# V's heads loaded alternately through SyncE's and ScalarE's queues

## Chip, cores, metric

One core of a Trainium2 chip. The metric is the device time of one execution in microseconds (us). Times inside a trace are us from the start of the span, which is what the profile covers of the execution; the span of the kernel before is 84.0 in an execution of 85.8. "Clock" is the clock that TensorE (PE in the views) was granted, as a share of its full speed.

## The reference

One decode step of a transformer block for 4 sequences: a layer norm whose scale and shift come from a condition, attention of 32 query heads over the last 1024 positions of a K and a V cache with 8 heads, and a feed-forward part, each with a residual.

```python
# B=4, D=512, Hq=32, Hkv=8, Dh=128, Dff=1792; W = 1024 positions of the cache are used
mod = (silu(c) @ w_mod).reshape(4, 6, 1, -1)           # sa, ca, ga, sb, cb, gb
h = layernorm(x) * (1 + ca) + sa
q = (h @ wq) as (B, Hq, 1, Dh)
p = softmax(q @ k[:, :, -W:].T * Dh ** -0.5)           # each K and V head serves 4 query heads
x = x + ga * ((p @ v[:, :, -W:]) as (B, 1, Hq*Dh)) @ wo
h = layernorm(x) * (1 + cb) + sb
x = x + gb * (relu(h @ w1) @ w2)
```

All inputs are bf16. K and V are 8 MB each, wq and wo 4 MB each, w_mod 3 MB, w1 and w2 1.75 MB each (MB of 2^20 bytes): 30.5 MB in all are read once for very little arithmetic.

## The kernel before

All large loads are written down first, all through SyncE's queue. K comes in eight tiles of 1 MB (k0 to k7), V in eight heads of 1 MB (v0 to v7). K and V share a pool of 11 buffers, so v3 and later need a buffer that a K tile has left. SyncE is not in the set of engines whose order is fixed by hand.

```python
ctx.enter_context(tc.manual_schedule(engines={PE, Activation, DVE, Pool}))        # names shortened
kvpool = ctx.enter_context(tc.tile_pool(name="kvpool", bufs=11))
...
nc.scalar.dma_start(out=cx_sb[0:B, :], in_=c)
nc.scalar.dma_start(out=cx_sb[B:2 * B, :], in_=A_x.rearrange("b o d -> (b o) d"))
... # through nc.sync: k0, k1, w_mod, wq (2 loads), k2 .. k7
for h in range(Hkv):
    vt_ = kvpool.tile([P, NI, Dh], bf16, tag="kv", name=f"v{h}")
    nc.sync.dma_start(
        out=vt_[:].rearrange("p j d -> p (j d)"),
        in_=A_v_cache[:, h, S - W:, :].rearrange("b (p j) d -> p b (j d)", j=NI),
    )
    v_tiles.append(vt_)
... # through nc.sync: wo (4 loads), w1, w2 (5 loads)
```

The compute stages that matter here, in the order of the text. `k_transposes` turns one K tile on TensorE and copies it out of PSUM (where this kernel has TensorE's results), two of four pieces on ScalarE and two on VectorE. The V products (`pv`) take the heads in the order 0 to 7 (the first three interleaved).

```python
for gi in range(KAHEAD, NG):                      # KAHEAD = 2, NG = 8
    if gi + 1 < NG:
        kts_pending.append(k_transposes(gi + 1))
    k_scores(gi, kts_pending.pop(0))
...
for iq in range(NQ):                              # four exponentials on ScalarE
    nc.scalar.activation(out=e_sb[:, ws]..., in_=sc_ps[:, ws]..., func=ACT.Exp, bias=nb[:], scale=scale, ...)
... # p_rep on VectorE; pT by TensorE, copied out half by ScalarE and half by VectorE
for iq in range(NQ):
    for h in range(VEARLY):                       # VEARLY = 3
        pv(h, iq * IQ, (iq + 1) * IQ, first=(iq == 0 and h == 0))
for h in range(VEARLY, Hkv):
    pv(h, 0, NI, last=(h == Hkv - 1))
... # o, products with wo, layer norm, products with w1 and w2, out
```

## Time and profile before

| | before |
|---|---|
| time, median of 4 runs | 85.91 us (85.75 to 86.06) |
| span of the profiled run | 84.0 us |
| mean rate over the span | 381 GB/s read from HBM |
| queue of SyncE / of ScalarE | 31.99 MB (of 10^6 bytes: the same 30.5) in 4196 packets / 0.01 MB in 16 packets |
| last large transfer done | near 80.1 us |
| last V product done | 62.73 us |

The table is read in one way: the transfers run without a gap from 2 us to 80 us (on the page the DMA share is 0.8 or more in every slice from 2.1 to 77.7, and the last chain is transfers for 92%), and the arithmetic follows them closely. The lines behind it are in the prediction.

### The profile page before, as it was taken

To read this page: it belongs to the slowest core of one execution; us is meant where nothing else is said; L and a number is where in the kernel's file an instruction comes from. 1 tells how busy PE (TensorE), PEld (TensorE's weight loads), DVE (VectorE), ACT (ScalarE), POOL (GpSimd) and SP (SyncE) were. 2 spreads that over 40 slices of the span, in tenths; PEclk is the share of its full clock that TensorE was granted. 3 is DMA by queue.
4 is the path that set the end of the run, shared out by engine and by line. 5 is a ranking of instruction groups with operands and counts; after the bars stand their busy time and mean duration, and the time that the engine had idled before them with its cause. 6 is when DMAs were issued, how large, how long until landed. Compare 5 with 4: busy or idle time off the path is not lost.

```text
span 84.0 us, 2368 instructions
## 1 busy us (share of the span) xinstructions
PE 57.2 (68%) x1064; PEld 46.8 (56%) x1064; DVE 26.3 (31%) x73; ACT 23.5 (28%) x37; POOL 5.2 (6%) x20
## 2 busy tenths in 40 slices
PE   0039930599629899999999239996455478598730
PEld 0039920238529749977777039996452058588510
DVE  0145470030430103654666677500003020241320
ACT  2314760003020004977789096300000010011000
POOL 6980000000000000000000000000000000000000
PEclk9999999858955555999999995795555555555555
DMA  0999998999989999999999999999999999999600
GB/s 2 329 406 452 456 480 374 429 444 429 437 374 417 417 441 409 409 413 433 425 406 413 425 429 417 409 425 429 413 409 413 429 419 443 417 376 401 236 4 2
DMA packets 4221, 32.14 MB, mean 382 GB/s; under 512 B 492, under 2 KB 628, under 8 KB 1140
## 3 DMA queue, kind: packets, MB, share of 16 engines
q1 hardware_dynamic: 4196, 31.99, 91.9%
q8 instruction: 8, 0.13, 0.6%
q10 hardware_dynamic: 16, 0.01, 0.0%
q14 instruction: 1, 0.01, 0.0%
HBM read 31.99 MB, written 0.00 MB: 381 GB/s over the span
## 4 chain that ended last, share of the span: by engine, by line
DMA 92%; SPq 2%; PE 1%; DVE 1%; issue 0%
DMA v<-in_A_v_cache_dram 28%; DMA wo_sb<-in_A_wo_dram 24%; DMA wq_sb<-in_A_wq_dram 21%; DMA w<-in_B_w_dram 19%; SPq L81 1%; PE z_ps L470 1%; SPq L90 1%; DVE zg L480 0%; DVE res L482 0%
## 5 line engine op out<-in xcount | busy, mean ns | idle before, releaser
L207 ACT COPY kT<-ktp 128x1024 bf16<-128x1024 bf16 x16 | 15.5, 1016 | 12.7 <-PE ktp L202 11.7
L202 PEld LDWEIGHTS <-k 128*128 128x128 bf16 x256 | 17.0, 108 | 3.7 <-issue 2.5
L202 PE MATMUL ktp<-ident_k,k 128*128 128x128 bf16 x256 | 18.0, 238 | 1.1 <-DMA k<-in_A_k_cache_dram 1.1
L205 DVE COPY kT<-ktp 128x1024 bf16<-128x1024 bf16 x16 | 11.1, 691 | 11.1 <-PE ktp L202 10.8
L340 PE MATMUL oT_ps<-pT,v 128*128 128x16 bf16 x256 | 7.3, 172 | 2.5 <-issue 1.9
L340 PEld LDWEIGHTS <-v 128*128 128x128 bf16 x256 | 7.1, 100 | 2.7 <-issue 2.0
L214 PE MATMUL sc_ps<-kT,qpad 128*32 128x512 bf16 x64 | 5.6, 445 | 0.4 <-DVE qpad L306 0.4
L357 PE MATMUL pT_ps<-ident_bf,p_rep 128*128 128x128 bf16 x32 | 3.3, 289 | 2.9 <-DVE p_rep L351 2.9
L357 PEld LDWEIGHTS <-p_rep 128*128 128x128 bf16 x32 | 2.9, 135 | 3.4 <-DVE p_rep L351 3.2
L236 PE MATMUL m_ps<-wmod_sb,siluT 128*32 128x512 bf16 x16 | 1.5, 516 | 4.5 <-DMA wmod_sb<-in_w_mod_dram 4.5
L302 PE MATMUL qT_ps<-hT,wq_sb 128*128 128x4 bf16 x128 | 3.6, 166 | 1.4 <-DVE ab L295 1.4
L302 PEld LDWEIGHTS <-wq_sb 128*128 128x128 bf16 x128 | 3.5, 104 | 1.5 <-issue 1.5
L409 ACT COPY y<-y_ps 128x256 f32<-128x256 f32 x1 | 0.4, 372 | 11.4 <-DVE y L408 11.4
L404 PE MATMUL y_ps<-wo_sb,o 128*32 128x512 bf16 x16 | 2.1, 620 | 2.0 <-DMA wo_sb<-in_A_wo_dram 1.1
L177 PE MATMUL tp<-ident_bf,cx_sb 8*128 8x8 bf16 x4 | 0.3, 167 | 4.5 <-DMA cx_sb<-in_A_x_dram 4.5
L236 PEld LDWEIGHTS <-siluT 128*32 128x32 bf16 x16 | 0.4, 107 | 4.8 <-issue 4.6
L382 DVE TENSOR_TENSOR oT_sb<-oT_ps,rb 128x128 bf16<-128x128 f32 x1 | 0.3, 292 | 8.6 <-PE oT_ps L340 8.6
L416 PEld LDWEIGHTS <-wo_sb 128*128 128x128 bf16 x64 | 2.5, 120 | 0.6 <-DMA wo_sb<-in_A_wo_dram 0.6
L416 PE MATMUL y_ps<-o,wo_sb 128*128 128x4 bf16 x64 | 2.4, 173 | 0.5 <-DMA wo_sb<-in_A_wo_dram 0.5
L351 DVE TENSOR_TENSOR p_rep<-e_sb,mi 128x512 int32<-128x512 int32 x4 | 2.5, 686 | 0.7 <-ACT e_sb L346 0.7
L470 PE MATMUL z_ps<-w,uT 128*32 128x128 bf16 x56 | 2.2, 302 | 0.7 <-DMA w<-in_B_w_dram 0.5
L177 PEld LDWEIGHTS <-cx_sb 8*128 8x128 bf16 x4 | 0.2, 108 | 4.5 <-issue 4.5
(107 smaller groups left out, 56.1 us busy)
## 6 DMA issues: line engine op xcount, KB each, us to landing
k<-in_A_k_cache_dram SPq DMA_DIRECT2D x8, 1024.0 KB, 26.2
v<-in_A_v_cache_dram SPq DMA_DIRECT2D x8, 1024.0 KB, 19.9
wq_sb<-in_A_wq_dram SPq DMA_DIRECT2D x2, 2048.0 KB, 20.7
wo_sb<-in_A_wo_dram SPq DMA_DIRECT2D x4, 1024.0 KB, 19.9
wmod_sb<-in_w_mod_dram SPq DMA_DIRECT2D x1, 3072.0 KB, 13.5
w<-in_B_w_dram SPq DMA_DIRECT2D x1, 1792.0 KB, 21.7
w<-in_B_w_dram SPq DMA_DIRECT2D x2, 512.0 KB, 19.2
w<-in_B_w_dram SPq DMA_DIRECT2D x1, 384.0 KB, 17.8
```

The lines of the kernel that those rows point to most:

```text
L202: nc.tensor.transpose(out=tp[:, ii, :], in_=k_tiles[gi][:, iq * IQ + ii, :], identity=ident_k)
L205: nc.vector.tensor_copy(out=dst, in_=tp[:])
L207: nc.scalar.copy(out=dst, in_=tp[:])
L214: nc.tensor.matmul(out=sc_ps[hw * CG:(hw + 1) * CG, half * HALF:(half + 1) * HALF], lhsT=qpad[:, b, par, hw, :], rhs=kT[:, half * (NI // 2 ...
L236: nc.tensor.matmul(out=m4_ps[k * CG:(k + 1) * CG, :], lhsT=siluT32[:, t, :], rhs=wmod_sb[:, t, k * D:(k + 1) * D], start=(t == 0), stop=(t ...
L302: nc.tensor.matmul(out=qT_v[:, hq, :], lhsT=wq_sb[:, t, hq * Dh:(hq + 1) * Dh], rhs=hT[:, t, :], start=(t == 0 and hq == 0), stop=(t == DT ...
L340: nc.tensor.matmul(out=oT_ps[:, hw, par].rearrange("p b r -> p (b r)"), lhsT=v_tiles[h][:, i, :], rhs=pT[:, i, c0:c0 + B * rep], start=(fi ...
L351: nc.vector.tensor_tensor(out=p_w[:, ws, :], in0=e_w[:, ws].unsqueeze(2).to_broadcast([P, WQ // 2, B]), in1=mi4[:].unsqueeze(1).to_broadca ...
L357: nc.tensor.transpose(out=tp[:, ii, :], in_=p_rep[:, i // 2, :, i % 2], identity=ident_bf[:])
L404: nc.tensor.matmul(out=y4_ps[q0:q0 + CG, :], lhsT=o4[:, l, g % 2, g // 2, :], rhs=wo_sb[:, g, l, :], start=(g == 0 and l < 4), stop=(g == ...
L416: nc.tensor.matmul(out=y_ps[:, m, :], lhsT=wo_sb[:, g, l, m::DT], rhs=o4[:, l, g % 2, g // 2, 0:B], start=False, stop=(g == NP - 1 and l = ...
L470: nc.tensor.matmul(out=z_ps[nh * CG:(nh + 1) * CG, :], lhsT=uT32[:, m, :], rhs=w2_sb[:, m, nh * DH2:(nh + 1) * DH2], start=(m == 0), stop= ...
```

## The change

The intent is to spread V's loads over two issuing engines. Even heads stay with SyncE, odd heads go to ScalarE. ScalarE's instructions are fixed in the order of the text, so its issues need places there: after the copies of k5, k6 and k7, and after the exponentials. SyncE joins the engines of fixed order, and the loads of wo, w1 and w2 move behind V in the text.

```diff
-        ... PE, Activation, DVE, Pool}))
+        ... PE, Activation, DVE, Pool, SP}))
     v_tiles = []
-    for h in range(Hkv):
+
+    def load_v(h, eng):
         vt_ = kvpool.tile([P, NI, Dh], bf16, tag="kv", name=f"v{h}")
-        nc.sync.dma_start(
+        eng.dma_start(
     ... (the loads of wo, w1, w2 leave this place)
     for gi in range(KAHEAD, NG):
         if gi + 1 < NG:
             kts_pending.append(k_transposes(gi + 1))
+
+        if gi >= NG - 4 and gi + 1 < NG:
+            h = 2 * (gi - NG + 4)
+            load_v(h, nc.sync)
+            load_v(h + 1, nc.scalar)
         k_scores(gi, kts_pending.pop(0))
     ... (after the four exponentials)
+    load_v(Hkv - 2, nc.sync)
+    load_v(Hkv - 1, nc.scalar)
+    ... (the loads of wo, w1, w2 unchanged, through nc.sync)
```

More of the change, by code (lines that the diff above doesn't have):

```diff
@@ L59 @@
     ctx.enter_context(tc.manual_schedule(engines={
-        mybir.EngineType.PE, mybir.EngineType.Activation, mybir.EngineType.DVE, mybir.EngineType.Pool}))
+        mybir.EngineType.PE, mybir.EngineType.Activation, mybir.EngineType.DVE, mybir.EngineType.Pool, mybir.EngineType.SP}))
     const = ctx.enter_context(tc.tile_pool(name="const", bufs=1))
@@ L109 @@
     NP = Hkv // 2
-    wo_sb = wts.tile([P, NP, NL, D], bf16, tag="big", name="wo_sb")
-    wo_src = A_wo.rearrange("(g p l) n -> p g (l n)", g=NP, l=NL)
-    wo_dst = wo_sb[:].rearrange("p g l n -> p g (l n)")
-    for g in range(NP):
-        nc.sync.dma_start(out=wo_dst[:, g, :], in_=wo_src[:, g, :])
-    w12 = wts.tile([P, DT * Dff + FT * D], bf16, tag="med", name="w12")
-    w1_sb = w12[:, 0:DT * Dff].rearrange("p (t n) -> p t n", t=DT)
-    w2_sb = w12[:, DT * Dff:DT * Dff + FT * D].rearrange("p (m n) -> p m n", m=FT)
-    nc.sync.dma_start(out=w1_sb, in_=B_w1.rearrange("(p t) n -> p t n", t=DT))
-    W2_CHUNKS = [(0, 4), (4, 4), (8, 3), (11, 2), (13, 1)]
-    assert sum(e for _, e in W2_CHUNKS) == FT
-    w2_dst = w12[:, DT * Dff:DT * Dff + FT * D]
-    for (m0, e) in W2_CHUNKS:
-        nc.sync.dma_start(out=w2_dst[:, m0 * D:(m0 + e) * D],
-                          in_=B_w2[m0 * P:(m0 + e) * P, :].rearrange("(q e) n -> q (e n)", e=e))
     nc.scalar.preload_act_table_set("natural_log_exp_and_others")
@@ L348 @@
                              bias=nb[:], scale=scale, accum_out=den4[:, iq:iq + 1])
+    load_v(Hkv - 2, nc.sync)
+    load_v(Hkv - 1, nc.scalar)
+    wo_sb = wts.tile([P, NP, NL, D], bf16, tag="big", name="wo_sb")
+    wo_src = A_wo.rearrange("(g p l) n -> p g (l n)", g=NP, l=NL)
+    wo_dst = wo_sb[:].rearrange("p g l n -> p g (l n)")
+    for g in range(NP):
+        nc.sync.dma_start(out=wo_dst[:, g, :], in_=wo_src[:, g, :])
+    w12 = wts.tile([P, DT * Dff + FT * D], bf16, tag="med", name="w12")
+    w1_sb = w12[:, 0:DT * Dff].rearrange("p (t n) -> p t n", t=DT)
+    w2_sb = w12[:, DT * Dff:DT * Dff + FT * D].rearrange("p (m n) -> p m n", m=FT)
+    nc.sync.dma_start(out=w1_sb, in_=B_w1.rearrange("(p t) n -> p t n", t=DT))
+    W2_CHUNKS = [(0, 4), (4, 4), (8, 3), (11, 2), (13, 1)]
+    assert sum(e for _, e in W2_CHUNKS) == FT
+    w2_dst = w12[:, DT * Dff:DT * Dff + FT * D]
+    for (m0, e) in W2_CHUNKS:
+        nc.sync.dma_start(out=w2_dst[:, m0 * D:(m0 + e) * D],
+                          in_=B_w2[m0 * P:(m0 + e) * P, :].rearrange("(q e) n -> q (e n)", e=e))
     for iq in range(NQ):
```

## The prediction

> **What bounds the kernel now.** I read the chain that ended last first, as the page sums it up and then in order of time (start, duration, what; all times in us from the span's start unless ns is said).
>
> ```profile
> DMA 92%; SPq 2%; PE 1%; DVE 1%; issue 0%
> ...
> 20.50 23.76 DMA v<-in_A_v_cache_dram
> ...
> 44.28 19.86 DMA wo_sb<-in_A_wo_dram
> ...
> 64.16 15.96 DMA w<-in_B_w_dram
> ```
>
> The end is set by transfers: 92% of the span is one chain of them. No engine is in it for over 2%. Next I read the span in four stretches (start:end, length, busy of PE, PEld, DVE, ACT, POOL with counts, PE clock, DMA share, GB/s).
>
> ```profile
> 20.50:44.30 23.80, 21.12 (x363) 17.31 (x364) 8.88 (x23) 10.15 (x13) 0.00 (x0) 0.78 1.01 419
> 44.30:64.20 19.90, 13.40 (x361) 11.95 (x358) 7.84 (x16) 6.13 (x13) 0.00 (x0) 0.74 1.01 419
> ```
>
> The transfer engines are full (share 1.0) at 419 GB/s while K's second part and V arrive. The bytes are the same after the change, so it can gain only if the rate rises. Then I read the issues in SyncE's queue, one window at a time (start, issue time).
>
> ```profile
> 4.41 0.60 SPq L81 DMA_DIRECT2D k<-in_A_k_cache_dram  x1
> 5.83 1.18 SPq L81 DMA_DIRECT2D k<-in_A_k_cache_dram  x2
> ...
> 20.50 0.54 SPq L101 DMA_DIRECT2D v<-in_A_v_cache_dram  x1
> 26.89 0.54 SPq L101 DMA_DIRECT2D v<-in_A_v_cache_dram  x1
> 29.37 0.54 SPq L101 DMA_DIRECT2D v<-in_A_v_cache_dram  x1
> 41.83 0.54 SPq L101 DMA_DIRECT2D v<-in_A_v_cache_dram  x1
> 44.28 0.33 SPq L114 DMA_DIRECT2D wo_sb<-in_A_wo_dram  x1
> ```
>
> An issue takes 0.54, but the next waits. v0 is issued at 20.50 and lands 23.76 later, at 44.26; wo's first part, the eighth load after v0, is issued at 44.28. So **a load is issued when the load eight places before it has landed**: there are eight in flight. In steady state one lands every 2.48 (26.89 to 29.37), which is 1.05 MB at 423 GB/s. By this rule k2 to k7 land at 29.37, 31.91, 34.38, 36.87, 39.36, 41.83, and v7 at 61.7. The count runs over both queues: k4 goes out at 5.83, when k0 lands, which is eight places back only if ScalarE's two small loads (c, x) are counted alternately with SyncE's, in the order c, k0, x, k1. That is an order planned by time, not the order of the text.
>
> Last, what TensorE does with the V heads and after (start, duration, in brackets the idle time before it and its releaser).
>
> ```profile
> 43.59 1.96 PE L202 MATMUL ktp<-ident_k,k 128*128 128x128 bf16 x32
> 45.48 1.25 PE L214 MATMUL sc_ps<-kT,qpad 128*32 128x512 bf16 x16
> 52.76 3.45 PE L340 MATMUL oT_ps<-pT,v 128*128 128x16 bf16 x128
> 61.71 1.02 PE L340 MATMUL oT_ps<-pT,v 128*128 128x16 bf16 x32 [0.59 <-DMA v<-in_A_v_cache_dram]
> 64.48 1.05 PE L404 MATMUL y_ps<-wo_sb,o 128*32 128x512 bf16 x8 [0.89 <-DVE o L395]
> 66.66 1.05 PE L404 MATMUL y_ps<-wo_sb,o 128*32 128x512 bf16 x8 [1.14 <-DMA wo_sb<-in_A_wo_dram]
> 71.64 1.23 PE L416 MATMUL y_ps<-o,wo_sb 128*128 128x4 bf16 x32 [0.48 <-DMA wo_sb<-in_A_wo_dram]
> 75.96 1.89 PE L459 MATMUL u_ps<-ab,w 128*128 128x8 bf16 x56 [0.43 <-DMA w<-in_B_w_dram]
> ```
>
> At every stage TensorE waits a little for data. Those waits are the slack in which a delay can be lost.
>
> [...] 0.54 of issue lies beside 2.48 of transfer, so there is no issue time to save. [...]
>
> **The change part by part.** *SyncE* loses four V loads and its order becomes that of the text: k0 to k7, v0, v2, v4, v6, wo, w1, w2. That costs nothing. *ScalarE* gains four issues. Its own two in the trace took 0.55 and 0.26; with 0.54 each that is 2.2, of which 1.6 lies in the K stage. There ScalarE copies 1.93 in every 2.48, which leaves 0.55, about one issue: hidden. *Bytes and rate* are unchanged: the last transfer still lands near 80.1, if the queues never run dry.
>
> *Order of arrival* is what moves. [...] v1 is reached soon after the two small activations at 24.4. Suppose first that the count follows the pairs (v0, v1, v2 ...). v1 then waits for wq's second half (26.89), v3 for k3, v5 for k5, v7 for k7. [...] the pair takes 2 x 2.48 = 4.96. Then: k2 and v1 at 31.85, k3 at 34.33, k4 and v3 at 39.29, k5 at 41.77, k6 and v5 at 46.73, k7 at 49.21. So **k7 lands 7.4 later**, behind three odd heads. From there:
> - k7's transposes to the last score took 3.14 (43.59 to 46.73): scores done at 52.4 (before 46.73, so +5.7; the 1.7 by which TensorE lagged behind k7 is taken up).
> - Scores to the first V product is 6.03 (46.73 to 52.76): 58.4. The V products without their waits are 5.35 + 1.08 + 1.02 = 7.45: done at 65.9, before 62.73. All V has landed by 61.7 as now, so these wait for nothing: **+3.2**.
> - The first wo product starts 1.75 later (67.65), and its two blocks take 2.1: 69.75 (before 67.71, +2.05, since wo's second part was waited for and now is not). To the second wo group 2.25, and that takes 2.42: 74.4 (before 72.87, +1.55).
> - w1's products could have started at 75.53 (75.96 less the wait 0.43): now 77.1, +1.1. The w2 products start at 79.15; 56 of them, at the 1.09 for 32 that the timeline has, take 1.9: 81.1, before 80.8.
>
> **Sum: +3.2 after V, less 2.9 of waits that are swallowed, +0.3 at the end: 86.3.**
>
> **Rivals.** *1. SyncE is ahead when the places are counted.* It waits for no compute, so if the planned order puts v2, v4, v6 and even wo ahead of v1, ScalarE's loads stand eight behind loads that land late. Example: v5 counted behind v4 and v7 behind wo's second part. By bytes, at 2.48 each from 41.83, v4 is the fifth or sixth (about 55.5) and wo's second the ninth (64.2). The exponentials stand behind v5 in ScalarE's stream: 55.5 and not 48.3. The copies of pT stand behind v7: 64.2; so the V products run to about 72.5, +9.8, less 2.6 of slack: about 93. For it: the count c, k0, x, k1 follows planned time. Against: the pairs stand in the text where the K stage has room, as if chosen so that the planned order is that of the pairs. *2. ScalarE does not run ahead*: v1, v3, v5 go out at about 41, 44, 46, K is not delayed, each pair shares, v6 and v7 land together at 61.7, the last head comes 1.0 later, and wo's wait of 1.14 swallows that: 86.0. [...] *3. Two queues move more*: [...]
>
> **Range and chances.** My main line with rivals 2 and 3 covers 85.4 to 87, weight about 0.6; rival 1 gives 88 to 94 by how far SyncE is ahead, weight somewhat over a third. No way gives 1.7 less, as the transfers were never idle: faster 0.04. The point is set between, nearer the main line: 87.0, range 85.6 to 92.5; same 0.58, slower 0.38.
>
> **What would show it.** Right: DMA share still 1.0 to 80 and the same GB/s; ScalarE's V issues at about 27, 34, 42, 49; k7's transposes near 49; V products without waits ending near 66; smaller waits for wo, w1 and w2. Wrong: ScalarE's issues at 41 or later (rival 2); ScalarE's exponentials or pT copies standing behind a load issue, or V products ending after 68 (rival 1); gaps in the DMA line[...].

## The result, and the profile after

A ratio below is the mean time of one kernel's fast runs over the mean of the other's fast runs of the same rounds, so it is not quite the ratio of the medians quoted.

The changed kernel took 87.92 us as the median of 4 runs (86.84 to 88.64) against 85.91. Two of the four count as slow (over 1.5% above the fastest run of the same kernel: 88.47 and 88.64); the two fast ones, 86.84 and 87.37, give **1.014 (95% interval 1.010 to 1.018)**. The same kernel was run again: 87.42 (86.62 to 87.73), ratio 1.019 (1.016 to 1.022). So it is 1 to 2% slower: five of its six fast runs are less than 2% above the 85.91 of before. Its runs scatter over 2 us; those of the kernel before scatter over 0.3.

The first profiled run of the change was slow (span 86.8, PE clock 0.70). I read the second profile, a fast one (span 84.8, clock 0.736; it is the profile of the first experiment below), against before. First the chain that ended last, from the page and in order of time:

```profile
PE 47%; DMA 37%; DVE 8%; issue 2%; SPq 1%; ACT 1%; DVEq 0%; ACTq 0%
...
48.58 17.45 DMA v<-in_A_v_cache_dram
66.08 1.04 PE oT_ps L327 x32
...
79.88 1.71 PE z_ps L478 x56
```

Before, 92% of this chain were transfers. Now the last of them is a V head (issued 48.58, landed after 17.45), and from 66.08 on the chain is arithmetic: TensorE no longer waits for wo, w1 or w2. The rate did not fall in the stretches that the prediction shows:

```profile
20.50:44.30 23.80, 21.13 (x364) 17.30 (x364) 8.88 (x23) 10.14 (x13) 0.00 (x0) 0.78 1.00 417
44.30:64.20 19.90, 12.38 (x297) 10.88 (x294) 7.08 (x13) 6.15 (x13) 0.00 (x0) 0.74 1.01 419
```

417 and 419 GB/s against 419 and 419. The same bytes move at the same rate; they arrive in another order. Next ScalarE's timeline (start, duration, what):

```profile
40.27 0.59 ACTq L102 DMA_DIRECT2D v<-in_A_v_cache_dram  x1
40.28 1.02 ACT L189 COPY kT<-ktp 128x1024 bf16<-128x1024 bf16 x1
...
42.77 0.54 ACTq L102 DMA_DIRECT2D v<-in_A_v_cache_dram  x1
45.21 0.54 ACTq L102 DMA_DIRECT2D v<-in_A_v_cache_dram  x1
48.30 0.47 ACT L333 ACTIVATE e_sb<-sc_ps,nb 128x256 bf16<-128x256 f32 x1 [2.08 <-DVE nb L310]
48.58 0.54 ACTq L102 DMA_DIRECT2D v<-in_A_v_cache_dram  x1
48.77 0.47 ACT L333 ACTIVATE e_sb<-sc_ps,nb 128x256 bf16<-128x256 f32 x1
```

v1 is issued 0.01 us before the copy ahead of it in ScalarE's order starts, that is, once this copy's wait for TensorE is over. v7, whose place is behind all four exponentials, goes out at 48.58, 0.19 before the second of them starts; the last three show no wait of their own in the trace. Of SyncE's issues one tells the order in which the places are counted:

```profile
41.83 0.33 SPq L343 DMA_DIRECT2D wo_sb<-in_A_wo_dram  x1
```

SyncE waited 1.8 for a K tile before it (k7, the last). So wo's first part stands eight places behind k7, where the pairs would have v7, and v7 is counted one place after it. Then what the two queues moved (packets, MB, share of the 16 engines), in windows 42 to 44, 44 to 46 and 54 to 58; q1 is SyncE's queue and q10 ScalarE's:

```profile
q1 hardware_dynamic: 113, 0.84, 101.2%
...
q10 hardware_dynamic: 59, 0.48, 57.9%
q1 hardware_dynamic: 56, 0.35, 42.6%
...
q10 hardware_dynamic: 116, 0.88, 52.7%
q1 hardware_dynamic: 113, 0.82, 49.1%
```

ScalarE's first data move at 44.1, 3.8 after the issue of v1. From then on each queue has half, up to the end of ScalarE's four heads. Last the V products on TensorE, which answer to those of before:

```profile
56.13 0.96 PE L327 MATMUL oT_ps<-pT,v 128*128 128x16 bf16 x32 [0.70 <-DMA v<-in_A_v_cache_dram]
61.10 1.87 PE L327 MATMUL oT_ps<-pT,v 128*128 128x16 bf16 x64 [2.66 <-DMA v<-in_A_v_cache_dram]
66.08 1.02 PE L327 MATMUL oT_ps<-pT,v 128*128 128x16 bf16 x32 [3.10 <-DMA v<-in_A_v_cache_dram]
68.84 1.90 PE L412 MATMUL y_ps<-wo_sb,o 128*32 128x512 bf16 x16 [0.88 <-DVE o L403]
```

The odd heads land 4.97 apart (56.1, 61.1, 66.1), twice the 2.48 of a load that has the engines to itself. The V products end at 67.10, 4.4 later than the 62.73 of before; the products with wo wait for no transfer any more. Of the 4.4, 3.6 are swallowed by such waits, and 0.8 are left in the span (84.8 against 84.0).

**The arithmetic of the last head.** ScalarE's 4 MB at half rate take 8 x 2.48 = 19.8; from 44.1 that is 63.9, and 2.1 later v7 has landed (66.05, when SyncE, whose next load was held for it, goes on). SyncE meanwhile moved its own heads and then, because its queue had nothing else, wo. Its issue of the third load of w2, which is held until wo's first part has landed, comes at 63.89, before v7. How much of wo passed v7 is an estimate from these times: k7 landed at 41.83 (wo's first issue waits for it), so its data ended near 39.7 (by the same 2.1); from there to 44.1 SyncE alone moved 4.4 / 2.48 = 1.8 MB of its V heads, with 2.2 MB left; of the 4 MB that it moved from 44.1 to 63.9, 1.8 were wo. 1.8 x 2.48 = 4.5, and v7's delay against before is 66.05 - 61.7 = 4.35.

**The scatter.** In the slow profiled run v1 goes out at 42.04, not at 40.27, its first data move at 45.8, v7 lands at 67.96 and the span is 86.8. So from the issue of v1 to the landing of v7 it is 25.9 there and 25.8 in the fast run. What differs comes before: in both, TensorE must finish the products with w_mod and wq and the turning of K until ScalarE gets to v1. Stretch 15.70 to 25.20 of before, of the slow run of the change, and of its fast run (PE clock, DMA share and GB/s are the last three columns):

```profile
15.70:25.20 9.50, 7.19 (x57) 4.89 (x58) 2.30 (x12) 1.24 (x4) 0.00 (x0) 0.70 1.00 424
```

```profile
15.70:25.20 9.50, 8.75 (x54) 6.12 (x54) 1.71 (x7) 0.73 (x2) 0.00 (x0) 0.50 1.00 423
```

```profile
15.70:25.20 9.50, 7.19 (x56) 4.78 (x56) 2.29 (x12) 1.24 (x4) 0.00 (x0) 0.70 0.99 422
```

At clock 0.50 this stage ends later, and v1 is issued 1.8 later. The runs without a profile agree. The eight runs of the changed kernel have spans of 84.8 and 85.1 at clocks of 0.736 and 0.737, 85.5 to 85.9 at 0.716 to 0.719, and 86.7 and 86.8 at 0.700; the kernel before has 84.0 to 84.3 at clocks from 0.706 to 0.740. That a low clock costs nothing where the transfers set the end is shown by the experiment two_heads below (span 84.1 at a clock of 0.50 in this stretch, against 84.1 at 0.68).

### The profile page after: what moved, and what is told of

Read it like the earlier page. It is cut to its first block, busy times and chain, and to the rows that moved or that the text cites.

```text
span 86.8 us, 2367 instructions
## 1 busy us (share of the span) xinstructions
PE 59.3 (68%) x1064; PEld 49.3 (57%) x1064; DVE 26.5 (31%) x73; ACT 23.6 (27%) x37; POOL 5.2 (6%) x20
## 4 chain that ended last, share of the span: by engine, by line
PE 48%; DMA 36%; DVE 8%; issue 2%; SPq 1%; ACT 1%; DVEq 0%; ACTq 0%
DMA v<-in_A_v_cache_dram 20%; DMA wmod_sb<-in_w_mod_dram 16%; PE ktp L184 14%; PE sc_ps L196 6%; PE qT_ps L284 4%; PE mT L235 2%; PE y_ps L424 2%; PE mT L237 2%; PE y_ps L412 2%; PE m_ps L218 2%; PE y_ps L420 2%; PE z_ps L478 2%; PE x_ps L440 1%; SPq L81 1%; DVE mx L308 1%
## 5 line engine op out<-in xcount | busy, mean ns | idle before, releaser
L420 PEld LDWEIGHTS y_ps<-sel_b,y 128*128 128x128 f32 x8 | 1.8, 328 | 1.4 <-DVE y L416 1.4
L196 PEld LDWEIGHTS <-qpad 128*32 128x32 bf16 x64 | 1.3, 103 | 2.2 <-DVE qpad L288 0.7
L232 ACT COPY m_sb<-m_ps 32x512 f32<-32x512 f32 x1 | 0.6, 576 | 6.9 <-PE m_ps L221 6.9
## 6 DMA issues: line engine op xcount, KB each, us to landing
w<-in_B_w_dram SPq DMA_DIRECT2D x1, 1792.0 KB, 17.7
```

The lines of the kernel that those rows point to most:

```text
L196: nc.tensor.matmul(out=sc_ps[hw * CG:(hw + 1) * CG, half * HALF:(half + 1) * HALF], lhsT=qpad[:, b, par, hw, :], rhs=kT[:, half * (NI // 2 ...
L420: nc.tensor.matmul(out=y_ps[:, t, :], lhsT=y4[:, t, :], rhs=sel_b[:], start=(t == 0), stop=False)
```

## The experiments

Theory T. Its first part was formed from the slow profile; the 3.6 comes from the fast one: *the loss is the late landing of ScalarE's heads. v7 lands 25.9 after v1 is issued, v1 is issued at ScalarE's turn, and a delay of the V products beyond 3.6 goes through to the end.* Rivals: R1, SyncE's new order or the places of the loads in the program; R2, ScalarE's time for the issues; R3, a cost of running two queues at all; and my own main line, K delayed by odd heads.

### The changed kernel again

> The changed kernel once more, to see both its states. Theory (late start): the end hangs on the moment at which ScalarE issues v1, which is its turn after the copies of k5; the last odd head lands some 25.9 us after that (3.8 until its first data, eight times 2.48 at half share, 2.3 until it has landed), and the end follows 16.2 later. So a run with a span of 85 has v1 issued near 40.3, one with 86.8 near 42.0. Rival (the slow runs are a state of the transfers): the same v1 issue in both, but a longer way from there to the end. Time 86.8 to 88.6.

Measured: 87.42 (86.62 to 87.73), ratio 1.019 (1.016 to 1.022); the profiled run had v1 at 40.27, v7 at 66.05, span 84.8. As T has it: 25.8 from issue to landing, at either clock. The three timed rounds (87.3 to 87.7) have no profile, so their issue times are not known; their mean clocks, 0.716 to 0.719 against 0.736, lie on the side that T asks for.

### All of V back in SyncE's queue, all else as changed

```diff
-            load_v(h + 1, nc.scalar)
+            load_v(h + 1, nc.sync)
-    load_v(Hkv - 1, nc.scalar)
+    load_v(Hkv - 1, nc.sync)
```

> The changed kernel with the four odd heads back in SyncE's queue, at the same places, SyncE still in the order of the text. Theory (ScalarE's heads land late): 85.9, ratio 1.00 against before, v7 landing near 61.7. Rival (SyncE's order, or the places of the loads in the program): 87 as after.

Measured: 85.95 (85.75 to 86.05), ratio 1.000 (0.998 to 1.002); last head at 61.68, span 84.1. R1 falls: the order and the places cost nothing; the loss is in the queue.

### Four small loads by ScalarE in place of the heads

```diff
-            load_v(h + 1, nc.scalar)
+            load_v(h + 1, nc.sync)
+            nc.scalar.dma_start(out=tiny[:, h // 2, :], in_=c)
```

> All of V through SyncE, and four loads of 4 KB (c again, into a tile that nobody reads) issued by ScalarE at the places of the odd heads. It keeps ScalarE's four issues of about 0.55 and takes their data away. Theory: 85.9 to 86.0, ratio 1.00. Rival (ScalarE's time for the issues is on the path): 86.5 to 87.

Measured: 86.31 (86.23 to 86.60), ratio 1.006 (1.004 to 1.008). Neither expectation fits exactly. In the trace V's products end at 62.78 and the store of the result is issued at 81.53, the same moment as in all_sync; the 0.3 of span (84.4 against 84.1) lies after that store is issued, where I have no explanation for it. The path to the result did not get longer, so R2 does not explain the change. One flaw of the test: a small issue takes 0.25, not 0.54, so it keeps only half of the issue time. The K stage itself bears the full ones: in the change the copies of k6 and k7 come at 41.86 and 44.30, in before at 41.85 and 44.29.

### Only two heads through ScalarE

```diff
-            load_v(h + 1, nc.scalar)
+            load_v(h + 1, nc.scalar if h < 4 else nc.sync)
-    load_v(Hkv - 1, nc.scalar)
+    load_v(Hkv - 1, nc.sync)
```

> Only v1 and v3 through ScalarE, at the places of the change; v5 and v7 back in SyncE's queue. Theory: first data of v1 about 44, two heads at half share are 9.9, landed about 56.3 to 58; SyncE's six heads are then the last, near 61.7: 85.9 to 86.2, ratio 1.00. Rival (a cost for each ScalarE issue, or for mixing two queues): half of the change's loss, 1.007 to 1.01.

Measured: 85.81 (85.75 to 85.85), ratio 0.999 (0.9975 to 1.0005), so no gain either. R3 falls: both queues are busy and nothing is lost. This profiled run also had the low clock, and its span is the same 84.1 as that of all_sync, which had 0.68 in this stretch:

```profile
15.70:25.20 9.50, 8.75 (x54) 6.11 (x54) 1.71 (x7) 0.73 (x2) 0.00 (x0) 0.50 0.98 416
```

```profile
58.16 0.97 PE L327 MATMUL oT_ps<-pT,v 128*128 128x16 bf16 x32 [0.89 <-DMA v<-in_A_v_cache_dram]
61.83 1.91 PE L327 MATMUL oT_ps<-pT,v 128*128 128x16 bf16 x66 [0.44 <-issue]
66.70 1.05 PE L412 MATMUL y_ps<-wo_sb,o 128*32 128x512 bf16 x8 [0.17 <-DMA wo_sb<-in_A_wo_dram]
```

v3 is ready at 58.16 (58.04 in the slow run of the change, with the same clock), but the last heads are back in SyncE's queue and their products start at 61.83; wo is waited for again.

### The loads one K tile later

```diff
-        if gi >= NG - 4 and gi + 1 < NG:
-            h = 2 * (gi - NG + 4)
+        if gi >= NG - 3:
+            h = 2 * (gi - NG + 3)
```

> The first three pairs one K tile later in the program than in the change (v1 after the copies of k6, v3 and v5 after those of k7), v7 unchanged. Theory (the end follows v1's issue): v1 issued about 42.7 (44.5 with the lower clock), the last odd head lands 25.9 later at 68.6, end 2.4 later than in the changed kernel of the same clock: span 87.2 to 89, time 89.0 to 90.9, ratio 1.035 to 1.055. Rival (the loss comes from the rate or from ScalarE's issue time): as the change, 1.015.

Measured: 89.02 (88.97 to 89.93), ratio 1.040 (1.034 to 1.046), span 87.1.

```profile
42.66 0.59 ACTq L102 DMA_DIRECT2D v<-in_A_v_cache_dram  x1
```

```profile
68.36 1.02 PE L327 MATMUL oT_ps<-pT,v 128*128 128x16 bf16 x32 [3.10 <-DMA v<-in_A_v_cache_dram]
```

v1 goes out 2.4 later than in the fast run of the change, v7 lands 2.3 later (25.7 after v1), the end comes 2.3 later. The end follows the issue one for one, as T says and R2 and R3 do not.

### The loads two K tiles earlier

```diff
-        if gi >= NG - 4 and gi + 1 < NG:
-            h = 2 * (gi - NG + 4)
+        if gi >= NG - 6 and gi + 2 < NG:
+            h = 2 * (gi - NG + 6)
     ... (the pair after the exponentials is now in the loop too)
```

> All pairs two K tiles earlier in the program (after the copies of k3, k4, k5, k6), still alternating between the queues. Theory: v1 is issued about 35.4, its first data moves about 39.2, the last odd head lands about 61.5, end as before: 85.9 to 86.3, ratio 1.00. Rival (two queues cost time in themselves, by their switching or by ScalarE's four issues): still 1.01 to 1.02.

Measured: 87.14 (85.84 to 87.54), ratio 1.006 (0.998 to 1.014) from its fast runs. The profiled run took 85.84, its three timed rounds 87.0 to 87.5, so the kernel has two kinds of runs, and the timed ones are not what T expected. In the profiled one the V products end at 64.88 and the span is 84.1. But the copies of k7 come at 47.39 and not at 46.06, as in the change at the same low clock: v7 now stands ahead of them in ScalarE's order and waits until 46.73 for v0, which is eight places before it in the count, to land. I took it up once more:

> early2 once more, because its profiled run took 85.84 and its three timed ones 87.0 to 87.5. Theory: the profiled one had the lower TensorE clock before 27 us and issued v1 at 37.4; with the higher clock v1 goes out near 34.9, so more of V comes ahead of k7 and v0, v7 (which waits for v0's landing) goes out later and holds the copies of k7 longer: exponentials near 54 in place of 51.3, end near 85.4 of span, time 87.2. If this run has v1 near 37.4 again, it should take 85.8 again. Rival: the same issue times with a different time.

Measured: 86.02 (two runs), ratio 1.001; v1 at 37.08, the low clock again, v7 held until 47.66, V products done at 66.19, span 84.2. The runs of 87 were not caught in a profile, so what made them stays open. The mean clocks fit the theory's direction, no more: 0.686 to 0.708 in the three runs with spans of 84.1 and 84.2, 0.714 to 0.732 in the three with 85.1 to 85.8.

### v1, v3, v5 two tiles earlier, v7 at its old place

```diff
-        if gi >= NG - 4 and gi + 1 < NG:
-            h = 2 * (gi - NG + 4)
+        if gi >= NG - 6 and gi + 3 < NG:
+            h = 2 * (gi - NG + 6)
```

> As early2 (v1, v3, v5 two K tiles earlier), but v7 at its old place after the exponentials, so that it does not hold up the copies of k7 while it waits. Theory: v1 issued 35.4 to 37.4, the odd heads land by about 61 to 63.5, end as before within 0.5: 85.9 to 86.4, ratio 1.000 to 1.006, and no rounds at 87 as early2 had. Rival (two queues cost time in themselves): 1.01 or more.

Measured: 85.90 (85.88 to 85.94), ratio 1.000 (0.999 to 1.002).

```profile
34.89 0.59 ACTq L102 DMA_DIRECT2D v<-in_A_v_cache_dram  x1
...
54.23 0.54 ACTq L102 DMA_DIRECT2D v<-in_A_v_cache_dram  x1
```

```profile
55.93 3.56 PE L327 MATMUL oT_ps<-pT,v 128*128 128x16 bf16 x128 [2.02 <-ACT pT L367]
65.02 1.02 PE L327 MATMUL oT_ps<-pT,v 128*128 128x16 bf16 x32 [0.85 <-DMA v<-in_A_v_cache_dram]
```

Alternating heads on two queues, with all of the change's issues, costs nothing if ScalarE's come early enough: R3 falls again. Two details were off. v7 waited for v2's landing until 54.23 and held ScalarE's copies of pT behind it, which cost TensorE 2.02; and it landed at 65.0, not by 63.5. The V products ended at 66.04, 3.3 later than before, and the end did not move.

### Odd heads between the K tiles, as my main line supposed

```diff
+    load_v(0, nc.sync)
+    load_v(1, nc.scalar)
     kts_pending.append(k_transposes(KAHEAD))
+    load_v(2, nc.sync)
+    load_v(3, nc.scalar)
     for gi in range(KAHEAD, NG):
-        if gi >= NG - 4 and gi + 1 < NG:
+        if gi == KAHEAD + 1:
     ... (loads v4 and v5 here; v6 and v7 stay after the exponentials)
```

> v1 just before the copies of k2 in ScalarE's stream, v3 after them, v5 after those of k4, v7 as in the change. This makes what the prediction's main line supposed: odd heads between the K tiles. By that line: v1 issued about 27 to 29, k7 landing 5 to 7 later than before (47 to 49), the V products done about 66, the end only 0.3 to 1 later than before: 86.2 to 87. If the delay of K is not swallowed: 89 or more.

Measured: 86.92 (86.76 to 87.16), ratio 1.012 (1.010 to 1.014), span 85.0.

```profile
26.75 0.59 ACTq L102 DMA_DIRECT2D v<-in_A_v_cache_dram  x1
```

```profile
48.84 1.96 PE L184 MATMUL ktp<-ident_k,k 128*128 128x128 bf16 x32 [2.48 <-DMA k<-in_A_k_cache_dram]
65.34 1.91 PE L330 MATMUL oT_ps<-pT,v 128*128 128x16 bf16 x66 [1.62 <-issue]
```

Here the supposed chain is real: k7 is ready at 48.8 (49.2 by the prediction's working), the V products end at 67.25 (65.9), and 1.0 of that reaches the end (0.3). The V products started on time, at 58.27 (58.4); what the working lacked is the pause of 1.62 in the last line shown. The kernel before has one of 1.92, up to 60.04, at the same place: two products before the end of v5. It is not a wait for V, as v5 is in use by then and v6 had landed at 59.2; the profile names no releaser. The working had taken it out with the waits. This chain is not what the change does. The run also shows that v1 could have gone out at 26.75: its own wait (wq's second half has landed) is the same in both kernels, so in the change it was held to 40.27 by nothing but its place behind the copies.

### Smaller pieces in SyncE's queue

In no run did ScalarE's first data move at once: for V heads 3.6 to 4.0 passed from issue to first data in all that I looked at (read in windows of 0.25; 3.8 to 3.9 in the fast run of the change, in windows of 0.1), and 3.2 to 3.5 for the first small load of tiny4. At the start of the span, with nothing ahead, it was 0.8 to 1.0 (before: c's load issued at 0.73, first data between 1.50 and 1.75). To see whether a number of pieces already taken up from SyncE's queue is ahead of them:

```diff
-        eng.dma_start(out=<v tile>, in_=<v head>)
+        for i in range(2 if h in (0, 2) else 1):        # v0 and v2 in two halves
+            eng.dma_start(out=<half of the v tile>, in_=<half of the v head>)
```

> The changed kernel with v0 and v2 each loaded as two halves on SyncE's queue, so that what stands in that queue when ScalarE issues v1 is in pieces of 4 KB and not 8 KB. In all runs so far v1's first data moved 3.7 to 3.8 after its issue. If what is ahead of it is a fixed number of pieces of SyncE's queue already taken up, the lag falls to about 2.2; if it is a fixed time or a fixed number of bytes, it stays at 3.7. The end would then be up to 1.5 earlier than the changed kernel of the same clock; not otherwise.

Measured: 86.56 (two runs), ratio 1.007 (1.004 to 1.010). v1 issued 40.17, first data at 44.07 or just after: 3.9 to 4.0, and the span is 84.7, against 84.8 of the change at the same clock. The pieces were halved as meant: from 42.4 to 43.0 SyncE's queue moved 0.24 MB in 64 packets, in the change 0.25 MB in 31. So it is not a number of pieces. Whether it is a time or a number of bytes stays open.

### All runs on one line

| run | v1 issued | last ScalarE head ready | V products done | span |
|---|---|---|---|---|
| before | - | - | 62.73 | 84.0 |
| all_sync | - | - | 62.70 | 84.1 |
| tiny4 | - | - | 62.78 | 84.4 |
| two_heads | 42.12 | 58.2 | 63.74 | 84.1 |
| early2 / again | 37.37 / 37.08 | not waited for alone | 64.88 / 66.19 | 84.1 / 84.2 |
| early2b | 34.89 | 65.0 | 66.04 | 84.1 |
| half_desc | 40.17 | 65.7 | 66.69 | 84.7 |
| change, fast run | 40.27 | 66.1 | 67.10 | 84.8 |
| early_k | 26.75 | not waited for | 67.25 | 85.0 |
| change, slow run | 42.04 | 68.0 | 69.01 | 86.8 |
| late1 | 42.66 | 68.3 | 69.38 | 87.1 |

Up to about 66.2 the span stays at 84.0 to 84.2 (but for tiny4, whose 0.3 lies elsewhere): the transfers cover the V products. From there on it is the end of the V products plus 17.7 to 17.8 (half_desc 18.0). This table is the result: the change moves the V products past the point where the transfers cover them. No version of it beats the kernel before.

## Why the prediction was right or wrong

The time (87.92 against 87.0, range 85.6 to 92.5) and the likelier class, "same", came out right; the mechanism did not. The 87.0 was set between a main line at 86.3 and a rival at 93, and neither of them happened, so that it lies so near is luck.

- **Bound by transfers before, bytes and rate unchanged: right.** 417 and 419 GB/s. In the changed kernel, though, the end is no longer set by transfers (37% of its last chain, 92% before).
- **Count over both queues, in the order of the pairs: right up to v6.** v2 waits for k2 (29.40), v4 for k4 (34.43), v6 for k6 (39.41). Then wo's first part comes ahead of v7 (41.83). That is rival 1's order for one load, and it cost nothing: v7 now waited for v0, which landed near 44.3, and it was issued at 48.58. The harm that rival 1 forecast did not occur in the change. In early2 and early2b it did in small: a load that waited for the count held ScalarE's copies (k7's in early2 to 47.39 in place of 46.06; pT's in early2b, for which TensorE waited 2.02).
- **"v1 is reached soon after the two small activations at 24.4": wrong, and this is the step that failed.** That ScalarE would get so far ahead was an assumption of mine that the trace of before did not show. It did not get ahead of the copy before the load; v1 went out at 40.27. This is rival 2, which I had at low weight. With it fell k7's delay of 7.4: k7 was on time, and the V products started at 52.78 (before 52.76).
- **Rival 2's own time, 86.0, was wrong too.** It let "each pair share, v6 and v7 land together at 61.7". Two terms were missing: the 3.8 until ScalarE's first data, and that SyncE's half of the engines goes to wo once its own four heads are through. Measured: v7 at 66.05. That a pair shares the engines evenly, which the trace of before could not show either, did occur (52.7% and 49.1%).
- **The slack: right in kind, somewhat small.** I had 2.9 swallowed out of 3.2, so 0.3 left; its V products lacked the pause described under the experiment with odd heads between the K tiles (1.62 there). The runs put the point at about 66.2, 3.5 after the 62.73 of before. In the changed kernel's fast run it was 4.4 less 3.6, so 0.8 left.
- **ScalarE's issue time hidden in the K stage: right.** The copies of k6 and k7 start within 0.01 of before.
- **No gain from two queues:** rival 3's higher rate, an assumption of mine that no trace had shown, did not occur (417 and 419 GB/s against 419 and 419), nor did the 85.4 that rested on it; even two_heads gives 0.999 (0.9975 to 1.0005).
- **Unforeseen: the clock.** Tying a load's issue to compute let TensorE's clock before 27 us reach the end here: two profiles of one kernel, with 0.50 and 0.70 from 15.70 to 25.20, differ by 2.0 in span, and 1.8 of it is there when v1 is issued.

## What to carry to other kernels

In this kernel, bound by transfers, a second queue added no bandwidth (417 to 419 GB/s in all); it took half from the first (52.7% and 49.1% from 54 to 58), and it took it from whatever the first would have sent in that time. So put on the second queue only what may arrive late, and issue it early enough. By the times of the change's fast run, the chain of loads there needed 3.8 until its first data (40.27 to 44.1), twice its size in transfer time (an odd head every 4.97, against 2.48), and, as estimated above, 2.1 until the last had landed (63.9 to 66.05). A load placed in ScalarE's stream went out at ScalarE's turn (v1 at 40.27; at 26.75 in early_k, where it stands ahead of the copies of k2), with all of the scatter of the work before it (40.27 and 42.04 in two runs of one kernel), and while it waited it held ScalarE up (v7 in early2, which held the copies of k7 to 47.39 in place of 46.06).
